# Scratch reads issued one unit behind the next write, and two norms ahead of two transposes, in a spectral filter with a gated MLP

## The chip, the cores and the metric

The kernel runs on one core of a Trainium2 chip. The metric is the device time of one execution in microseconds. The core has five instruction queues: PE (TensorE, matmuls), DVE (VectorE), ACT (ScalarE), POOL (GpSimd) and SP (SyncE, which here only issues DMAs). Each queue executes its own instructions in order and waits on semaphores for the others. An instruction that waits holds up everything behind it on its queue, also DMAs that have nothing to wait for.

## The reference

An input x of 2048 rows and 512 columns is layer-normed, and two branches of the normed input are added to x: a filter in the frequency domain (two-dimensional real FFT, product with complex weights, inverse FFT) and an MLP with a gated GELU of width 1792.

```python
def _A_ref(x, w_r, w_i):
    B, S, D = x.shape
    X = jnp.fft.rfft2(x.astype(jnp.float32), axes=(-2, -1))
    X = X * (w_r + 1j * w_i)
    return jnp.fft.irfft2(X, s=(S, D), axes=(-2, -1)).astype(jnp.bfloat16)

def _B_ref(x, w_gate, w_up, w_down):
    g = jnp.einsum("bsd,df->bsf", x, w_gate)
    u = jnp.einsum("bsd,df->bsf", x, w_up)
    h = _gelu(g) * u
    return jnp.einsum("bsf,fd->bsd", h, w_down)

x = A_x
xn = _layernorm(x, axis=-1)
return x + _A_ref(xn, A_w_r, A_w_i) + _B_ref(xn, B_w_gate, B_w_up, B_w_down)
```

## The kernel before

The rows are handled as 16 tiles of 128, in four blocks b of four tiles. The MLP is the backbone of TensorE's program: for each block and each of 14 chunks fc of the width there are a gate group (L685, four matmuls), an up group (L700, four matmuls), a GELU on ACT (L688) and a product on DVE (L706) into hT. The down products (L738, 14 matmuls for a tile) of a block run between the groups of the next block.

The spectral branch is threaded into this backbone by hand. A counter of hooks runs along the MLP groups; plan maps a hook's number to calls, and at(h, call) enters one. When the MLP loop reaches a hook, the calls of that number write their instructions into the queues. So the order within every queue is the order of the hooks, and all queues see the same order. PSUM banks are given out by take, from modelled times of TensorE and ACT.

The spectral branch has these stages. D units (the FFT over columns) and A units (first half of the FFT over rows) write their result to scratch memory in DRAM (scr1), and load_tv reads it back transposed into tv. Eight B units (the second half of the FFT, L570), each with a product with the filter weights W on DVE (L581), are followed by eight C units (first half of the inverse over rows, L595). A C unit ends with an eviction on ACT (L600) into one of two buffers vp, and a DMA on SP that writes vp to the scratch tensor scr2 (256 KB, L602). load_vv(g) (L605) is the DMA on SP that reads unit g back into vv, in the order that the last stage needs; vv lies in the same memory as the matrices of the first stages, the arena. It waits for its own unit's write to have landed. Every E unit (the second half of the inverse over rows, L619) needs all eight parts of vv. F units (L649), the inverse over columns, follow, and the results are added to x_sb and written out.

B unit g stands at hook 60 + 4.6 g, rounded down, and C unit g - 1 at the same hook. The E units begin at hook 113.

SP also issues the loads of the imaginary filter weights W_i in that stage (L337, function load_late): eight units, four DMAs for each, with W buffers for four units; those of the last four units fall among the C units (hooks 67, 68, 72, 73, 76, 77, 81, 82). Each waits for TensorE's progress at its hook and for the multiplies that last read the buffer. A small side path, mini, treats column 256; its step 3 at hook 100 sends a 4 KB row to scratch position z256 by a DMA on SP.

At the start, x tiles and the first weights come in by DMAs on the SP and ACT queues, which wait for nothing. The first two tiles are handled singly, so that the first gate can begin early: ln_stat and ln_aggr (statistics on DVE, a power on POOL with the constant tile mhalf, L388), ln_norm (L392, DVE) into xn, and trans1: for each half of the columns two transposes on TensorE (L832) and a copy from PSUM into xnT, the first half on DVE (L839), the second on ACT (L841). The first gate reads both tiles of xnT.

Of the kernel before, what the change touches and what calls it, by code (L numbers as in the profile page):

```python
# [11 lines left out]
F32 = mybir.dt.float32  # L12
# [6 lines left out]
P = 128  # L19
# [195 lines left out]
def bass_parallel_sum__spectral_gfnet__glu_gated_geglu__prompt_kernel(  # L215
# [27 lines left out]
    with ExitStack() as es:  # L243
        def sb(name, shape, dt):
            return es.enter_context(nc.sbuf_tensor(name, shape, dt))
# [50 lines left out]
        gl = [sb("gl%d" % i, [P, 512], BF16) for i in range(3)]  # L296
        st = sb("st", [P, NJ, 6], F32)
        ag = sb("ag", [P, NJ, 2], F32)
        vpe = sb("vpe", [P, NJ], F32)
        mhalf = sb("mhalf", [P, 4], F32)  # L300
        rstd = sb("rstd", [P, NJ], F32)
        dumm = sb("dumm", [P, 512], F16)
        warm_o = sb("warm_o", [P, 1], F32)
# [7 lines left out]
        def bank_h(i):  # L311
            return psum_h[:, i * 1024:(i + 1) * 1024]
# [8 lines left out]
        def take(n, dur, hold=None, ops=1):  # L321
            i = min(range(9 - n), key=lambda i: max(free[i:i + n]))
            pt[0] += dur
            if hold is None:
                act_t[0] = max(act_t[0], pt[0] + 0.25) + 0.2 + 0.43 * n
                end = act_t[0]
            else:
                end = pt[0] + hold
            for k in range(i, i + n):
                free[k] = end  # L330
            return i
# [50 lines left out]
        def ln_aggr(j0, n):  # L382
            for j in range(j0, j0 + n):
                op("dve", lambda e, j=j: e.bn_aggr(ag[:, j, :], st[:, j, :]), r=[("st", j)], w=[("ag", j)])
            sl = slice(j0, j0 + n)
            js = range(j0, j0 + n)
            op("dve", lambda e: e.tensor_scalar(vpe[:, sl], ag[:, sl, 1], LN_EPS, None, ALU.add), r=[("ag", j) for j in js], w=[("vpe", j) for j in js])  # L387
            op("pool", lambda e: e.tensor_tensor(rstd[:, sl], vpe[:, sl], mhalf[:, 0:n], ALU.pow), r=[("vpe", j) for j in js] + ["mhalf"],  # L388
               w=[("rstd", j) for j in js])

        def ln_norm(j):
            op("dve", lambda e: e.tensor_scalar(xn[:, j % 4, :], x_sb[:, j, :], ag[:, j, 0:1], rstd[:, j:j + 1], ALU.subtract, ALU.mult),  # L392
               r=[("x", j, 0), ("x", j, 1), ("ag", j), ("rstd", j)], w=[("xn", j % 4)])
# [365 lines left out]
        def at(h, *calls):  # L759
            plan.setdefault(int(h), []).extend(calls)  # L760
# [40 lines left out]
        for m in range(4):  # L801
            h = (11, 22, 31, 39)[m]
# [6 lines left out]
        for g in range(9):  # L809
            h = int(60 + 4.6 * g)  # L810
            if g < 8:
                at(h, (unit_B, g))
            if g > 0:
                at(h, (unit_C, g - 1))
                at(h + 3, (load_vv, g - 1))
            if g == 1:
                at(h, (mini, 1))
            if g == 8:
                at(h - 2, (mini, 4))
                at(h, (mini, 2))  # L820
        at(100, (mini, 3))
        for j in range(NJ):
            at(113 + 2.2 * j, (unit_E, j))
            at(117 + 2.2 * j, (unit_F, j))

        def trans1(j):
            for i, eng in enumerate(("dve", "act")):
                bk = take(1, 0.12, 1.0)
                def f(e, i=i, bk=bk):
                    ins = None  # L830
                    for a in range(2):
                        ins = e.transpose(bank_h(bk)[:, a * P:(a + 1) * P], xn[:, j, (2 * i + a) * P:(2 * i + a + 1) * P], ident[:])  # L832
                    return ins
                op("pe", f, r=["ident", ("xn", j)], w=[("ps", bk)])
                dst = xnT[:, 2 * i:2 * i + 2, j * P:(j + 1) * P]
                src = bank_h(bk)[:, 0:256].rearrange("p (a c) -> p a c", a=2)
                ks = [("xnT", 0, 2 * i + a, j) for a in range(2)]
                if eng == "dve":
                    op("dve", lambda e, dst=dst, src=src: e.tensor_copy(dst, src), r=[("ps", bk)], w=ks)  # L839
                else:  # L840
                    op("act", lambda e, dst=dst, src=src: e.activation(dst, src, ACT.Copy), r=[("ps", bk)], w=ks)  # L841
# [3 lines left out]
        ln_stat(1)  # L845
        ln_aggr(0, 2)
        ln_norm(0)
        trans1(0)
        ln_norm(1)
        trans1(1)  # L850
        gate(0, 0, (0, 1))
        ln_stat(2)
# [82 lines left out]
```

## Time and profile before

| | us |
|---|---|
| median of five runs | 189.76 |
| lowest and highest of the five | 188.70, 193.11 |
| the profiled execution: its own time | 189.76 |
| the profiled execution: span of the profile | 188.0 |

The granted TensorE clock was 1.00 in every stretch read. The stretches around the change:

| stretch, us | what runs in it | PE busy, us | ACT busy, us | DVE busy, us | DMA share |
|---|---|---|---|---|---|
| 6.5 to 8.5 | norm and transposes of the first two tiles | 0.78 | 0.77 | 0.90 | 1.09 |
| 8.5 to 13.5 | first gates and ups | 4.09 | 1.92 | 3.84 | 1.11 |
| 76 to 96 | B and C units, first half | 20.00 | 10.21 | 11.10 | 0.75 |
| 96 to 110 | B and C units | 14.00 | 7.46 | 7.61 | 0.86 |
| 110 to 122 | last B and C units | 11.95 | 6.58 | 5.74 | 0.72 |
| 122 to 134 | MLP alone, last scratch write and read | 12.00 | 3.25 | 4.31 | 0.47 |
| 134 to 181 | E and F units | 47.00 | 23.36 | 33.62 | 0.17 |

The busy time of an engine is the time that its records cover. Matmuls are pipelined, so their records overlap. The DMA share is the mean busy share of the core's 16 DMA engines; it can exceed 1 where packets of several queues overlap. In the lines of a timeline the first number is the start, the second the length, then the engine and line, what is written from what, and the number of instructions; a bracket gives the idle time of the engine ahead of it and what ended it. SPq is the issue of a DMA by SP, not its transfer.

### The profile page before, as it was taken

Reading aid. Unit: us, or ns where it says so; the run is one execution under the profiler, and the core shown is the slowest. Engines: PE = TensorE matmul, PEld = TensorE weight load, DVE = VectorE, ACT = ScalarE, POOL = GpSimd, SP = SyncE. Lnnn points to the kernel's source line nnn. Section 1 sums busy time; section 2 is a strip of 40 time slices with the busy share of each in tenths; the row PEclk is TensorE's granted clock in tenths of the full one; section 3 lists DMA queues with packets and bytes.
Section 4 is the critical chain, followed back from the end, with each engine's and each line's share of the span. In section 5 each row is a group of like instructions: output and inputs, shape, how many; then the busy total and the mean of one; then the engine's idle time right before and its main releaser. Section 6 shows DMA issues by size and latency. Waiting matters only on the chain.

```text
span 188.0 us, 3473 instructions
## 1 busy us (share of the span) xinstructions
PE 179.4 (95%) x1284; PEld 95.4 (51%) x1284; DVE 110.9 (59%) x262; ACT 88.8 (47%) x143; POOL 40.8 (22%) x90
## 2 busy tenths in 40 slices
PE   7589999999999999999999999999999999999991
PEld 2368655565655444444444444444555555555460
DVE  3566989997352242446635555423259879699520
ACT  1334547766566431456734555413265566654100
POOL 2110081824000007634654311000011111110000
PEclk9999999999999999999999999999999999999999
DMA  4999999788979249658988977664002212211111
GB/s 123 278 236 287 316 253 303 222 158 150 189 108 165 43 107 148 132 140 197 192 137 168 146 139 128 115 120 99 4 0 56 56 45 70 58 36 25 28 42 42
DMA packets 24977, 24.71 MB, mean 131 GB/s; under 512 B 2832, under 2 KB 22800, under 8 KB 24704
## 3 DMA queue, kind: packets, MB, share of 16 engines
q1 hardware_dynamic: 20992, 18.24, 47.2%
q0 software_dynamic: 1968, 5.14, 11.6%
q10 hardware_dynamic: 2000, 1.11, 2.2%
q8 instruction: 10, 0.16, 0.4%
q14 instruction: 7, 0.06, 0.1%
HBM read 18.19 MB, written 6.29 MB: 130 GB/s over the span
## 4 chain that ended last, share of the span: by engine, by line
PE 67%; DMA 16%; DVE 8%; SPq 4%; issue 2%; ACT 2%; POOL 1%; DVEq 0%; ACTq 0%
PE ps L738 21%; PE ps L700 18%; PE ps L685 17%; DMA scr<-early 10%; DMA wu<-in_B_w_up_dram 5%; DVE st L380 3%; SPq L334 2%; PE ps L649 2%; PE ps L619 2%; SPq L337 2%; DVE hT L706 1%; PE ps L402 1%; DMA out_dram<-x_sb 1%; ACT early L600 1%; PE ps L471 1%
## 5 line engine op out<-in xcount | busy, mean ns | idle before, releaser
L706 DVE TENSOR_TENSOR hT<-ps,gl 128x512 bf16<-128x512 f32 (+1 forms) x62 | 39.2, 637 | 34.5 <-PE ps L700 26.4
L700 PE MATMUL ps<-xnT,wu 128*128 128x512 f16 (+1 forms) x248 | 58.6, 359 | 1.0 <-DMA wu<-in_B_w_up_dram 0.9
L685 PE MATMUL ps<-xnT,wg 128*128 128x512 f16 (+1 forms) x248 | 58.6, 359 | 0.6 <-ACT xnT L841 0.6
L688 ACT ACTIVATE gl<-ps 128x512 bf16<-128x512 f32 (+1 forms) x62 | 34.3, 556 | 42.5 <-PE ps L685 41.3
L738 PE MATMUL ps<-wd,hT 128*128 128x512 bf16 x210 | 49.1, 380 | 0.0
L685 PEld LDWEIGHTS ps<-xnT,wg 128*128 128x128 bf16 x248 | 23.4, 98 | 21.7 <-issue 1.9
L700 PEld LDWEIGHTS ps<-xnT,wu 128*128 128x128 bf16 x248 | 23.4, 98 | 21.3 <-DMA wu<-in_B_w_up_dram 1.2
L738 PEld LDWEIGHTS ps<-wd,hT 128*128 128x128 bf16 x210 | 19.7, 98 | 21.9 <-issue 1.0
L640 DVE TENSOR_TENSOR x_sb<-ps,x_sb 128x512 bf16<-128x512 f32 (+1 forms) x17 | 11.2, 660 | 20.9 <-PE ps L738 17.5
L337 POOL DMA_DIRECT2D W<-in_A_w_r_dram x32 | 18.6, 612 | 12.0 <-PE ps L685 7.8
L628 POOL COPY tv<-tv 1x128 bf16<-1x128 bf16 x16 | 4.5, 284 | 51.7 <-ACT tv L626 51.7
L581 DVE TENSOR_TENSOR early<-early,W 128x1024 bf16<-128x1024 f16 x16 | 10.4, 688 | 6.8 <-ACT early L576 6.8
L655 ACT ACTIVATE tv<-ps 128x512 bf16<-128x512 f32 x16 | 9.5, 595 | 9.8 <-PE ps L649 9.8
L380 DVE BATCH_NORM_STATS2 st<-x_sb 128x6 f32<-128x512 bf16 x16 | 10.5, 683 | 2.9 <-DMA x_sb<-in_A_x_dram 2.9
L447 ACT ACTIVATE early<-ps 128x512 f16<-128x512 f32 x16 | 9.5, 595 | 5.4 <-PE ps L443 5.4
L576 ACT ACTIVATE early<-ps 128x1024 f16<-128x1024 f32 x8 | 8.2, 1023 | 6.1 <-PE ps L570 6.1
L626 ACT ACTIVATE tv<-ps 128x512 bf16<-128x512 f32 x16 | 9.6, 598 | 3.0 <-PE ps L619 3.0
L600 ACT ACTIVATE early<-ps 128x1024 bf16<-128x1024 f32 x8 | 8.2, 1022 | 4.6 <-DMA scr<-early 4.6
L479 ACT ACTIVATE early<-ps 128x1024 f16<-128x1024 f32 x8 | 7.9, 1021 | 4.6 <-PE ps L474 3.8
L388 POOL TENSOR_TENSOR rstd<-vpe,mhalf 128x4 f32<-128x4 f32 (+1 forms) x5 | 4.5, 901 | 23.5 <-DVE vpe L387 23.5
L559 POOL COPY w<-W 128x4 bf16<-128x4 bf16 x16 | 5.2, 355 | 14.4 <-DMA W<-in_A_w_i_dram 14.4
L392 DVE TENSOR_SCALAR cmx<-x_sb,ag,rstd 128x512 f16<-128x512 bf16 x16 | 6.2, 423 | 2.1 <-POOL rstd L388 2.1
(75 smaller groups left out, 147.5 us busy)
## 6 DMA issues: line engine op xcount, KB each, us to landing
W<-in_A_w_r_dram POOLq DMA_DIRECT2D x32, 64.2 KB, 3.9
W<-in_A_w_i_dram SPq DMA_DIRECT2D x32, 64.2 KB, 4.7
tv<-scr SPq DMA_DIRECT2D x8, 256.0 KB, 5.5
scr<-early SPq DMA_DIRECT2D x8, 256.0 KB, 4.2
arena<-scr SPq DMA_DIRECT2D x8, 256.0 KB, 4.3
out_dram<-x_sb SPq DMA_DIRECT2D x30, 64.0 KB, 2.0
scr<-early SPq DMA_DIRECT2D x14, 128.0 KB, 3.4
x_sb<-in_A_x_dram SPq DMA_DIRECT2D x6, 256.0 KB, 11.9
```

The costliest lines, as they stand in the source:

```text
L337: op(eng, lambda e: e.dma_start(dst, src), w=list(keys) + list(also), dma=True, after=[("pe", pr.cnt["pe"])])
L380: op("dve", lambda e: e.bn_stats(st[:, j, :], x_sb[:, j, :]), r=[("x", j, 0), ("x", j, 1)], w=[("st", j)])
L447: op("act", lambda e: e.activation(x4.rearrange("p (a c r) -> p a c r", a=2, r=4), bank(bk).rearrange("p (a r c) -> p a c r", a=2, r=4), A ...
L581: op("dve", lambda e, k=k: e.tensor_tensor(pp[i][k], xc[i], W[k][g % 4][:, :, :, 0:256], ALU.mult), r=[("xc", i)] + [key for c in range(2) ...
L600: op("act", lambda e: e.activation(vp[i].rearrange("p c hh k -> p (c hh k)"), pair(bk), ACT.Copy), r=[("ps", bk), ("ps", bk + 1)], w=[("vp ...
L626: op("act", lambda e: e.activation(z, bank(bk).rearrange("p (a c) -> p a c", a=4), ACT.Copy, scale=SC_E), r=[("ps", bk)], w=[zk] + (TVK if ...
L640: op("dve", lambda e: e.tensor_tensor(x_sb[:, j, cs], src, x_sb[:, j, cs], ALU.add), r=r + [("acc", j), ("x", j, 0), ("x", j, 1)], w=[("ac ...
L685: ins = e.matmul(bank(bg)[:, 0:n], wg_sb[:, dc, fc * P:(fc + 1) * P], xnT[:, dc, c0:c0 + n], start=(dc == 0), stop=(dc == 3))
L688: op("act", lambda e: e.activation(gl[k % 3][:, 0:n], bank(bg)[:, 0:n], ACT.Gelu_apprx_tanh), r=[("ps", bg)], w=[("gl", k % 3)])
L700: ins = e.matmul(bank(bu)[:, 0:n], wu_sb[:, dc, fc * P:(fc + 1) * P], xnT[:, dc, c0:c0 + n], start=(dc == 0), stop=(dc == 3))
L706: op("dve", lambda e: e.tensor_tensor(hT[b % 2][:, fc, h0:h0 + n], bank(bu)[:, 0:n], gl[k % 3][:, 0:n], ALU.mult), r=[("ps", bu), ("gl", k ...
L738: ins = e.matmul(bank(bk), hT[b % 2][:, fc, jj * P:(jj + 1) * P], wd_sb[:, fc, :], start=(fc == 0), stop=(fc == NFC - 1))
```

## The change

Three edits. The allocation of the small tile mhalf moves ahead of that of vpe. In the plan, the read of unit g - 1 at three hooks behind C unit g - 1 goes; in its place the read of unit g - 2 is entered at the hook of C unit g - 1, after it, and the read of the last unit is entered at hook 101. At the start, ln_norm(1) is issued ahead of trans1(0).

```diff
@@ -296,8 +296,8 @@
         st = sb("st", [P, NJ, 6], F32)
         ag = sb("ag", [P, NJ, 2], F32)
+        mhalf = sb("mhalf", [P, 4], F32)
         vpe = sb("vpe", [P, NJ], F32)
-        mhalf = sb("mhalf", [P, 4], F32)
         rstd = sb("rstd", [P, NJ], F32)
@@ -812,13 +812,15 @@
                 at(h, (unit_B, g))
             if g > 0:
                 at(h, (unit_C, g - 1))
-                at(h + 3, (load_vv, g - 1))
+                if g > 1:
+                    at(h, (load_vv, g - 2))
             if g == 1:
                 at(h, (mini, 1))
             if g == 8:
                 at(h - 2, (mini, 4))
                 at(h, (mini, 2))
         at(100, (mini, 3))
+        at(101, (load_vv, 7))
         for j in range(NJ):
             at(113 + 2.2 * j, (unit_E, j))
             at(117 + 2.2 * j, (unit_F, j))
@@ -845,8 +847,8 @@
         ln_stat(1)
         ln_aggr(0, 2)
         ln_norm(0)
+        ln_norm(1)
         trans1(0)
-        ln_norm(1)
         trans1(1)
         gate(0, 0, (0, 1))
         ln_stat(2)
```

## The prediction

> **What bounds the kernel now.** I read the busy shares first, then the slices of the span.
>
> ```profile
> PE 179.4 (95%) x1284; PEld 95.4 (51%) x1284; DVE 110.9 (59%) x262; ACT 88.8 (47%) x143; POOL 40.8 (22%) x90
> ...
> PE   7589999999999999999999999999999999999991
> ```
>
> TensorE is busy everywhere but in the first 14 us and the last 6. Matmul records overlap, so a busy row can hide small holes. I therefore looked for holes in the distance between starts in TensorE's timeline: four 512-column matmuls of a gate or up group take 0.86 us from start to start of the next group. After 8.5 us, four gate or up groups end in a wait: 1.11 us at 12.45, 0.39 at 25.9, 0.23 at 33.8 and 0.22 at 120.3. The change can only win what it takes out of these, out of the 8.5 us ahead of the first gate, or out of the tail.
>
> Then the chain that ended last, which seems to contradict this:
>
> ```profile
> PE 67%; DMA 16%; DVE 8%; SPq 4%; issue 2%; ACT 2%; POOL 1%; DVEq 0%; ACTq 0%
> PE ps L738 21%; PE ps L700 18%; PE ps L685 17%; DMA scr<-early 10%; DMA wu<-in_B_w_up_dram 5%; DVE st L380 3%; SPq L334 2%; PE ps L649 2%; PE ps L619 2%; SPq L337 2%; DVE hT L706 1%; PE ps L402 1%; DMA out_dram<-x_sb 1%; ACT early L600 1%; PE ps L471 1%
> ```
>
> It gives 10% (18.5 us) to the scratch writes of the inverse. This follows one release, of 0.22 us, back through a string of transfers that ran beside a full TensorE. The 18.5 us are what the string lasts, not what it costs. SP's timeline shows why it is a string: each read (arena<-scr) waits for the write just ahead of it to land, and the next write stands behind that read.
>
> ```profile
> 115.21 0.42 SPq L334 DMA_DIRECT2D scr<-early  x1
> 119.40 0.30 SPq L334 DMA_DIRECT2D arena<-scr  x1
> 119.75 0.42 SPq L334 DMA_DIRECT2D scr<-early  x1
> 124.05 0.30 SPq L334 DMA_DIRECT2D arena<-scr  x1
> 124.40 0.42 SPq L334 DMA_DIRECT2D scr<-early  x1
> 128.56 0.30 SPq L334 DMA_DIRECT2D arena<-scr  x1
> ```
>
> One turn is 4.5 us. What it delays: ScalarE may not evict a C unit (L600) until the write of two units earlier has landed; it waits three times, 4.6 us in all, and TensorE feels only the last, for a PSUM bank.
>
> ```profile
> ACT early L600 <- DMA scr<-early: 4.6, 3, 2.6
> ...
> 119.47 1.03 PE L685 MATMUL ps<-xnT,wg 128*128 128x512 f16 x4
> 120.55 1.04 PE L700 MATMUL ps<-xnT,wu 128*128 128x512 f16 x4
> ```
>
> 1.08 - 0.86 = **0.22 us**. And the last read, issued at 128.56, takes 4.4 us, so it lands at 132.96; the first E unit loads its weights at 133.13. The string ends 0.17 us before TensorE needs it.
>
> **Part 1, the reads one unit behind.** Eight reads (0.31 us of SP each) and eight writes stay; no instruction is added. The read of unit g-1, which stood three hooks behind its write, now stands behind the write of unit g, a full turn of 4 or 5 hooks (about 5 us) later, and waits for a write that is by then mostly down. SP's queue is then write 1, read 0, W loads, write 2, read 1, and so on. Working it out from ScalarE's L600 starts plus 1.02 us: write 3 can go at 99.6 (before: 104.2), write 4 at 105.0 (111.3), write 7 at about 118.7 (124.4). Read 7 now also stands behind the z256 row's DMA, whose row is ready at 121.96, and needs write 7 landed: 118.7 + 4.2 = 122.9. It lands at 127.3, **5.8 us** ahead of the first E unit instead of 0.17. L600 loses its 4.6 us of waits. The gain at TensorE is the 0.22 us alone: next late is TensorE itself.
>
> Moved past: the two W_i loads at hooks 68, 73, 77 and 82 no longer queue behind a read that waits for a fresh write. They issue up to some 4 us earlier (today the second pair for unit 6 issues at 101.9, behind the read at 101.56, and GpSimd's copy of it waits until 109.3). They keep their own waits: TensorE's progress and the multiplies that free the W buffers. None of today's multiplies (L581) is put down to a W load in the waits, so that is worth nothing at TensorE. A read that still waits would hold up the next write and W pair on SP; that is less than today's full landing each time. The first read overwrites the arena's matrices, last read at 62.7, so it waits for nothing there.
>
> Two rules of the Trainium skill differ from rows here. "DMA: Bandwidth & Descriptors", Anatomy of one DMA, fits a transfer (on GpSimd's path) at 2.0 us plus its bytes at 436 GB/s. My estimate from it is 2.6 us for 256 KB; a turn would be about 3.3 us, SP would always be back in time, and this part would gain 0. The rows have 2.6 to 5.4 us for these writes, six of eight above 4, so I take the row: 0.22. The same page, Issuing engines are not separate DMA queues, speaks against the change: all queues run on the same 16 engines and interleave, so a read let loose beside a write brings no bandwidth, and both may land later. At worst, both landings double. The stretches of the windows view say how near that is: DMA share 0.86 at 96 to 110, 0.72 at 110 to 122, 0.47 at 122 to 134. The end decides, where there is room, so I take no growth, and keep doubling for the rival below.
>
> **Part 2, both norms ahead of the transposes.** Two DVE instructions swap with one copy; nothing is added. Today DVE runs norm 0, copy, norm 1, copy:
>
> ```profile
> 6.03 0.41 DVE L392 TENSOR_SCALAR cmx<-x_sb,ag,rstd 128x512 f16<-128x512 bf16 x1 [0.85 <-POOL rstd L388]
> ...
> 7.11 0.40 DVE L392 TENSOR_SCALAR cmx<-x_sb,ag,rstd 128x512 f16<-128x512 bf16 x1
> ```
>
> Two norms in a row take 0.83 us (the pair at 24.33), so norm 1 ends at 6.86 instead of 7.51. Transposes follow 0.15 later, 7.0 to 7.4; ScalarE's second copy (0.38) runs 7.43 to 7.81, and the first gate, 0.15 behind it, starts at 7.96 instead of 8.53: **0.57 us**. TensorE then runs into the weights. A gate or up group of 256 columns takes 0.435. The third gate could start at 9.70, but its weights, issued at 3.19, land after 6.7 us, at 9.9; the fifth gate's land at 4.12 + 7.6 = 11.7. And the fifth up:
>
> ```profile
> 12.02 0.60 PE L685 MATMUL ps<-xnT,wg 128*128 128x256 f16 x4
> 13.56 0.61 PE L700 MATMUL ps<-xnT,wu 128*128 128x256 f16 x4 [0.94 <-DMA wu<-in_B_w_up_dram]
> ```
>
> It waits for wu 4 to 6, issued at 4.67, landed at 13.51. These loads wait for no computation, so nothing in this part moves them. The hole grows from 1.11 us to about 1.4, and **0** of the 0.57 is left. If the cover is gone, all 0.57 comes through. The swapped 16- and 64-byte allocations move two small operands of five pow instructions; no row prices an address. Between 0 and, say, doubling the one pow on the chain (1.02 us at 23.29), I take 0, since the instructions keep shape and type.
>
> **Sum.** The profiled execution took 189.76 us: 188.0 of span and 1.76 around it. 188.0 - 0.22 - 0 = 187.8; with 1.76, **189.5 us**. Its 189.76 is also the median of the five runs, which spread from 188.70 to 193.11. I count 0.5% (0.95 us) as what a measurement of this kernel can tell from no change.
>
> **Rivals.**
>
> *A typical execution waits where this one just doesn't* (faster; 0.35). The string's end had 0.17 us to spare, and from 96.26 to 132.96 it consists almost wholly of landings. If these are 4% longer in another execution, the string ends 1.5 us later and TensorE waits 1.3 us at the first E unit. The change takes this wait away. For it: the spread of the five times, two of them above 192. Against it: the profiled execution has the median's time with no such wait, and the spread can as well come from the weight loads at the start. Its time: the lowest of the five, with the least waiting, less 0.22: 188.5.
>
> *The start's gain comes through* (0.10). 189.76 - 0.22 - 0.57 = 189.0, still within 0.5%. It needs wu 4 to 6 landed before 12.1 us; DMA share is above 1 from 6.5 to 13.5, which speaks against it.
>
> *The freed transfers crowd each other* (slower; 0.05). At 118.7 write 7 goes, and the first E unit starts 133.1 - 118.7 = 14.4 us later; write and read need 8.6 us today. Above 14.4, that is at 1.7 times today's landings, TensorE waits for the difference: doubled, 17.2 us, 2.8 us late, 189.76 - 0.22 + 2.8 = 192.3. The DMA share of 0.47 there speaks against it.
>
> *Something else makes it slower by over 0.5%* (0.06): an address, or later weight landings, about 191.
>
> *No gain that shows*, my forecast: 0.44.
>
> **How the numbers follow.** Faster 0.35; same 0.44 + 0.10 = 0.54; slower 0.05 + 0.06 = 0.11. Predicted 189.5. The range runs from 187.8 (the first rival with another 0.4%) to 190.6 (the forecast plus 0.6% of spread), which leaves the slower cases out. The forecast's own range is 188.6 to 190.4.
>
> **What would show it.** Right: writes and reads alternate on SP with reads of the unit before, write 7 issues near 119, the last read lands near 127, L600's wait for scr is gone, and the 0.22 us hole at 120.3 with it; the first gate starts near 8.0 and the fifth up still near 13.5. Wrong: landings of scr above 7 us in the changed kernel, a hole ahead of the first E unit, a fifth up much before 13.2, or a median gain above 1 us, which would mean that the profile before was a lucky execution.

## The result, and the profile after

The changed kernel takes 188.87 us (median of 40 runs, 187.85 to 190.05); the kernel before, in the same comparison, 189.66 us (77 runs, 188.62 to 193.11). The ratio is **0.9962, with a 95% interval of 0.9948 to 0.9976**: 0.7 us less, between 0.45 and 1.0. Ratios here and below leave out the executions that are more than 1.5% above the fastest of the same kernel. The forecast was a gain of 0.2 us, within the 0.5% that the text called no change; the measured one (0.4%) stays within it too, but is three times as large and clear of nothing.

The profiled execution of the changed kernel has a span of 187.2 us and a time of 188.97. Its busy shares and slices:

```profile
PE 180.1 (96%) x1284; PEld 95.5 (51%) x1284; DVE 110.8 (59%) x262; ACT 88.9 (47%) x143; POOL 39.7 (21%) x90
...
PE   7889999999999999999999999999999999999991
```

TensorE is the bound as before. The chain that ended last has lost its scratch writes:

```profile
PE 81%; DVE 8%; DMA 6%; SPq 2%; issue 2%; POOL 1%; ACT 0%; DVEq 0%
PE ps L738 25%; PE ps L700 22%; PE ps L685 21%; DMA wu<-in_B_w_up_dram 4%; DVE st L380 3%; SPq L334 2%; PE ps L595 2%; PE ps L619 2%; PE ps L649 2%; PE ps L570 1%; DVE hT L706 1%; PE ps L402 1%; DMA out_dram<-x_sb 1%; PE ps L471 1%; PE ps L721 1%
```

The 10% that stood at "DMA scr<-early" are now TensorE's, and the span is 0.8 us shorter, not 18.5: the share said what the string lasted. SP's timeline at the end of the inverse (start, length of the issue, what is issued):

```profile
118.25 0.36 SPq L334 DMA_DIRECT2D scr<-early  x1
118.65 1.25 SPq L334 DMA_DIRECT2D arena<-scr  x1
121.22 0.59 SPq L334 DMA_DIRECT2D tv<-row  x1
121.86 0.58 SPq L334 DMA_DIRECT2D arena<-scr  x1
```

The last write goes at 118.25 and the last read at 121.86; with its 4.4 us it lands at 126.3, and the first E unit loads its weights at 132.33. No wait of the evictions L600 for scr is listed any more, and TensorE's timeline runs through where the hole was:

```profile
ACT early L600 <- PE ps L595: 0.8, 1, 0.8
...
118.92 1.03 PE L685 MATMUL ps<-xnT,wg 128*128 128x512 f16 x4
119.78 1.03 PE L700 MATMUL ps<-xnT,wu 128*128 128x512 f16 x4
```

0.86 us from start to start, where it was 1.08. At the start of the kernel:

```profile
7.81 0.60 PE L685 MATMUL ps<-xnT,wg 128*128 128x256 f16 x4 [0.59 <-ACT xnT L843]
...
13.00 0.61 PE L700 MATMUL ps<-xnT,wu 128*128 128x256 f16 x4 [0.90 <-DMA wu<-in_B_w_up_dram]
```

The fifth up still waits for its weights, but these landed at 13.0, not at 13.5. The span fell by 0.8 us: 0.56 at the fifth up and 0.22 at the hole. Are these 0.56 us the change's doing, or the luck of one execution?

For the profiles below the span can be taken apart in the same way. From the start of the fifth up to the end, 174.2 us pass where no wait for SP's string is left in TensorE's timeline: 174.20 in the changed kernel (187.2 - 13.00), and 174.1 to 174.3 in the other profiles without such a wait and with the same tail. What a profile has above that agrees to about a tenth with the holes that end in such a wait. So each profile gives two numbers, the start of the fifth up and what is above 174.2, here called the string's toll.

### The profile page after: what moved, and what is told of

The parts are those of the page before. It is cut to its first block, busy times and chain, and to the rows that moved or that the text cites. A ratio compares the mean times of both kernels' runs of the same rounds, so it can differ in the third digit from the quotient of the medians.

```text
span 187.2 us, 3473 instructions
## 1 busy us (share of the span) xinstructions
PE 180.1 (96%) x1284; PEld 95.5 (51%) x1284; DVE 110.8 (59%) x262; ACT 88.9 (47%) x143; POOL 39.7 (21%) x90
## 4 chain that ended last, share of the span: by engine, by line
PE 81%; DVE 8%; DMA 6%; SPq 2%; issue 2%; POOL 1%; ACT 0%; DVEq 0%
PE ps L738 25%; PE ps L700 22%; PE ps L685 21%; DMA wu<-in_B_w_up_dram 4%; DVE st L380 3%; SPq L334 2%; PE ps L595 2%; PE ps L619 2%; PE ps L649 2%; PE ps L570 1%; DVE hT L706 1%; PE ps L402 1%; DMA out_dram<-x_sb 1%; PE ps L471 1%; PE ps L721 1%
## 5 line engine op out<-in xcount | busy, mean ns | idle before, releaser
L600 ACT ACTIVATE early<-ps 128x1024 bf16<-128x1024 f32 x8 | 8.2, 1020 | 0.8 <-PE ps L595 0.8
L640 DVE TENSOR_TENSOR x_sb<-tv,x_sb 128x512 bf16<-128x512 bf16 x16 | 6.8, 425 | 0.6
```

The source lines that it names most:

```text
L640: op("dve", lambda e: e.tensor_tensor(x_sb[:, j, cs], src, x_sb[:, j, cs], ALU.add), r=r + [("acc", j), ("x", j, 0), ("x", j, 1)], w=[("ac ...
```

## The experiments

**Each part alone, and the kernel before once more.** Three runs with one part each, and one of the kernel before, unchanged:

```diff
# reads_only
-                at(h + 3, (load_vv, g - 1))
+                if g > 1:
+                    at(h, (load_vv, g - 2))
...
         at(100, (mini, 3))
+        at(101, (load_vv, 7))
# norms_only
-        trans1(0)
         ln_norm(1)
+        trans1(0)
# alloc_only
+        mhalf = sb("mhalf", [P, 4], F32)
         vpe = sb("vpe", [P, NJ], F32)
-        mhalf = sb("mhalf", [P, 4], F32)
```

> The kernel before with the moved scratch reads alone. Theory S (the start's gain comes through in most executions, the reads give what the hole at 120.3 had): 0.2 us less than before, a ratio near 0.999, the hole at 120.3 gone, wu 4 to 6 awaited as before. Theory R (most executions wait in the inverse stage longer than the profiled one, and the reads take that away): 0.6 to 0.7 us less, a ratio near 0.9965. Theory A (the addresses of two small tiles): 0.2 us less, as under S.

> The kernel before with both norms ahead of the transposes alone. Theory S: about 0.5 us less, a ratio near 0.9972; the first gate near 7.9 and the fifth up nearer to 13.0 than to 13.5. Theory R: no difference in the time, ratio 1.000, the first gate near 7.9 and the fifth up at about 13.5. Theory A: no difference.

> The kernel before with the allocation of mhalf ahead of that of vpe alone. Theories S and R: no difference, ratio 1.000. Theory A: some 0.5 us less, ratio near 0.997.

> The kernel before, unchanged, as a second sample of its profile and as a measure of what a comparison can tell. All theories: ratio 1.000. Theory R expects a profile in which the first E unit or a C unit's eviction costs TensorE more than the 0.22 us of the first profile; theory S expects about 0.2 us there again, and a landing of wu 4 to 6 that differs from 13.5 by some tenths.

| kernel | median, us | ratio to before, 95% interval | time of the profiled execution | fifth up starts | string's toll |
|---|---|---|---|---|---|
| before | 189.66 | | 189.76 | 13.56 | 0.24 |
| reads alone | 189.14 | 0.9965, 0.9942 to 0.9987 | 189.17 | 13.20 | 0 |
| norms alone | 190.12 | 1.0016, 0.9986 to 1.0047 | 190.53 | 13.05 | 1.45 |
| allocation alone | 189.41 | 0.9987, 0.9962 to 1.0012 | 190.01 | 13.72 | 0.28 |
| before, again | 189.72 | 0.9995, 0.9969 to 1.0022 | 188.90 | 12.79 | 0.1 |
| both parts | 188.87 | 0.9962, 0.9948 to 0.9976 | 188.97 | 13.00 | 0 |

Theory R has the better of it: the moved reads alone have a gain clear of nothing (0.25 to 1.1 us), and at its central value it is the whole of it. Theory S, in the form in which the norms give half a microsecond by themselves, fails in the time, though it had the start right (the fifth up nearer to 13.0). That they give something once the reads are moved is left open by it. Theory R missed on the second profile of before: it expected a toll above 0.22, and there is about 0.1 and no hole near 120. The allocation shows no effect.

The spread gives a hint how the reads gain. In before, a tenth of the executions lie below 188.84 and a tenth above 190.80; with moved reads the two bounds are 188.80 and 190.40, and the median is 0.5 us lower. The best executions are as they were, the middle and the long ones are shorter. This fits a string that takes something in some executions and nothing in others. Two columns of the table say more on the start. The fifth up starts between 12.79 and 13.72 without the norms' change, so the 13.00 of the changed kernel is within what the weights' landing does from one execution to the next. In the second profile of before, the weights, issued at 4.7, had landed after 7.9 us, by 12.6, and the fifth up did not wait at all:

```profile
12.35 0.60 PE L685 MATMUL ps<-xnT,wg 128*128 128x256 f16 x4
12.79 0.60 PE L700 MATMUL ps<-xnT,wu 128*128 128x256 f16 x4
```

Then TensorE itself is the limit, and an earlier first gate would pay.

The surprise is in the profile of the norms alone. Its fifth up is half a microsecond earlier than in the first profile, and it loses more than that near 120. TensorE's timeline there, then SP's where the string falls behind:

```profile
119.33 1.03 PE L685 MATMUL ps<-xnT,wg 128*128 128x512 f16 x4
121.34 0.82 PE L700 MATMUL ps<-xnT,wu 128*128 128x512 f16 x3 [0.99 <-ACT early L600]
```

```profile
102.83 1.00 SPq L334 DMA_DIRECT2D scr<-early  x1
103.93 1.26 SPq L337 DMA_DIRECT2D W<-in_A_w_i_dram  x2
110.37 0.31 SPq L334 DMA_DIRECT2D arena<-scr  x1
```

Write 3 was issued 1.4 us earlier than in before (102.83 against 104.20), yet the read that waits for it stands at 110.37 instead of 109.66. All later writes are late by about that, the evictions on ScalarE wait 7.6 us for scr instead of 4.6, and the hole that this tears in TensorE is 1.15 us instead of 0.22. The rest of the toll of 1.45 is a second hole: the late eviction also holds up the GELU behind it on ScalarE, and a C unit that waits for this starts at 112.59, 0.34 us after TensorE could have started it.

```profile
ACT early L600 <- DMA scr<-early: 7.6, 3, 3.1
...
112.01 0.41 PE L570 MATMUL ps<-tv,be 64*64 64x256 f16 x8
112.59 0.63 PE L595 MATMUL ps<-early,cmx 64*64 64x256 bf16 x16 [0.16 <-ACT gl L688]
```

**The norms alone, once more.** The same edit, to see whether that was one execution.

> The norms alone once more, for a second profile and a larger sample. Theory T (the span is the start of the fifth up, plus a constant, plus what SP's string of writes and reads takes from TensorE; the norms pay only where the weights land early): fifth up near 13.0, no hole near 120 as large as the 1.15 us of the first profile, a time between 0 and 0.4 us below the kernel before, and a few executions below 188.6. Theory G (the string gives back what the start gains): a hole near 120 above 0.5 us again, no execution below 188.6, ratio 1.000 or above.

189.48 us, ratio 0.9991 (0.9961 to 1.0021). Its profile is nearly the same, line by line: write 3 at 102.88, its read at 110.35, and near 120:

```profile
119.30 1.03 PE L685 MATMUL ps<-xnT,wg 128*128 128x512 f16 x4
121.19 1.04 PE L700 MATMUL ps<-xnT,wu 128*128 128x512 f16 x4 [0.86 <-ACT early L600]
```

The fifth up at 13.02, a toll of 1.4. No execution of the 14 was below 188.6, and none of the 14 of the first run. Theory T, which expected no such hole and a few executions below 188.6, fails. Theory G fits both profiles: with the reads where they were, the string gave back what the start had gained. Both profiled executions are above the medians of their runs (190.53 against 190.12, 190.42 against 189.48), so a typical toll is smaller. Nor does an earlier start always bring a hole: the second profile of before started its fifth up earlier still, at 12.79, and had none. Why write 3 lands so late when the norms are moved was not settled; the string's toll may depend on how its transfers meet the W loads around 102 to 110, but no run shows it.

**A third eviction buffer.** If the toll is the C unit's eviction, which waits for a buffer, a third buffer takes it away without touching the reads.

```diff
# vp3
+        vp.append(sb("vp2", [P, 1024], BF16)[:].rearrange("p (c hh k) -> p c hh k", c=2, hh=2))
...
-            op("act", lambda e: e.activation(vp[i]...), r=[...], w=[("vp", i)])
+            op("act", lambda e: e.activation(vp[g % 3]...), r=[...], w=[("vp", g % 3)])
...
-            dma("sp", ..., vp[i]..., r=[("vp", i)], w=[("scr2", g)])
+            dma("sp", ..., vp[g % 3]..., r=[("vp", g % 3)], w=[("scr2", g)])
# vp3_late: as vp3, and
-            at(113 + 2.2 * j, (unit_E, j))
-            at(117 + 2.2 * j, (unit_F, j))
+            at(115 + 2.2 * j, (unit_E, j))
+            at(119 + 2.2 * j, (unit_F, j))
# before_E_first: the kernel before, and
-            at(113 + 2.2 * j, (unit_E, j))
-            at(117 + 2.2 * j, (unit_F, j))
+            at(111 + 2.2 * j, (unit_E, j))
+            at(115 + 2.2 * j, (unit_F, j))
```

> The kernel before with a third buffer for the evictions of the C units, reads as before. Theory C (what typical executions lose is TensorE's wait for a bank that a C unit's late eviction holds, near 120): L600 no longer waits for scr, the hole near 120 is gone, and most of the gain of the moved reads is there, 0.4 to 0.7 us, ratio 0.9965 to 0.998. Theory E (they lose it at the first E unit, which waits for the last read): SP's string of writes and reads is as long as before, so no gain, ratio 1.000, and a wait ahead of the first E unit in some executions.

189.54 us against 189.53, ratio 1.0006 (0.9978 to 1.0034). In the profile the hole near 120 is gone, and so is the toll; the last read is issued at 128.16, nearly as late as before, from a first write at 96.34 (before: 96.26), so the string is about as long as it was. Its fifth up starts at 14.14, later than in any other profile with this order of loads. The gain of 0.4 us or more that theory C asked for isn't there, and neither is the wait at the first E unit that theory E expected in some executions. That is the other place where the string can take its time, so I tried both edges:

> The kernel before with a third eviction buffer and the E and F units two hooks later, reads as before. Theory O (the string takes its time from TensorE at two places, the C unit's late eviction near 120 and the first E unit; with one closed it takes it at the other): with both closed the gain of the moved reads is there, 0.5 to 0.7 us, ratio about 0.9965. Theory E0 (the string takes nothing that these two places can show, and the moved reads gain elsewhere): ratio 1.000, as with the third buffer alone.

> The kernel before with the E and F units two hooks (one gate and one up, 1.73 us) earlier. Theory O: the last read lands when it did, so TensorE waits ahead of the first E unit for 1.2 to 2.5 us, and the time rises by about that much, ratio 1.006 to 1.013. Theory E0 (the first E unit had room to spare in typical executions): a wait of at most 1 us, ratio below 1.004.

The third buffer with later E units: 189.30 us against 189.80, ratio 0.9993 (0.9960 to 1.0026). Both 0.9965 and 1.000 lie in that interval; it doesn't tell the two theories apart. Its profile has neither a hole near 120 nor a wait at the first E unit.

E units two hooks earlier: 191.13 us, **ratio 1.0058 (1.0026 to 1.0090)**, 1.1 us more (0.5 to 1.7) for 1.73 us of advance. That lies between what the two theories called for, at the lower edge of theory O. My estimate from it is that in a typical execution of before the string ended about 0.6 us ahead of the first E unit (1.73 - 1.1), with an interval of 0 to 1.2 us, if the wait there is all that the earlier units cost; the first profile had 0.17. The profiled execution of this run took 192.55 us, 1.4 above the median; it shows where the string bites, not how hard in a typical execution:

```profile
121.93 1.04 PE L700 MATMUL ps<-xnT,wu 128*128 128x512 f16 x4 [1.36 <-ACT early L600]
132.10 1.03 PE L700 MATMUL ps<-xnT,wu 128*128 128x512 f16 x4
134.37 0.38 PE L619 MATMUL ps<-be,arena 128*128 128x128 f16 x4 [1.24 <-DMA arena<-scr]
```

The second wait is made by the edit. The first isn't: at 121.9 the kernel is still instruction for instruction the one before. So a long execution of before can have a hole of 1.5 us there. The other four profiles with the old reads, the old eviction and the old norms (before, before again, allocation alone, and the one with early weights below) had 0.22, 0, 0.31 and 0, the two with the norms alone 1.15 and 1.03. The profiles with moved reads, five of them with those below, have none near 120 and none at the first E unit.

**The cover at the start.** The norms' gain was to be hidden by the weights of chunks 4 and 5. I tried to bring these in earlier, half of them on ACT's queue:

```diff
# before_early, reads_early, after_early
             load_w(t, v, nm, 2, 4, eng)
+            load_w(t, v, nm, 4, 6, eng)
...
-        load_w(wg_sb, wgv, "wg", 4, 6, "sp")
-        load_w(wu_sb, wuv, "wu", 4, 6, "sp")
```

> The kernel before with the weights of chunks 4 and 5 issued right behind those of 2 and 3, half of them on ACT's queue. Theory W (the fifth up waits for its weights in most executions): wu 4 to 6 lands before 12.5, the fifth up starts near 12.5, and the time falls by what the wait had, some 0.5 to 0.9 us. Theory G (the inverse's string of transfers is paced by itself, so an earlier start only makes the hole near 120 larger): no gain in the time, a hole larger by what the start gained.

> The moved reads and the early weights, norms as before. Theory W: the gains add up, 1.2 to 1.6 us less than before, ratio near 0.993. Theory G, since the string is gone here: the same.

> The changed kernel with the early weights. If the weights' landing is what covers the norms' gain, it shows here: up to 0.57 us less than the kernel with moved reads and early weights but norms as before, a ratio near 0.990, fifth up near 11.9. If the norms give nothing even without that cover, it is equal to that kernel.

| kernel | median, us | ratio to before, 95% interval | executions below 188.6 us |
|---|---|---|---|
| before + early weights | 190.21 | 1.0028, 1.0000 to 1.0055 | 0 of 22 |
| moved reads + early weights | 189.30 | 0.9988, 0.9966 to 1.0009 | 1 of 22 |
| both parts + early weights | 189.22 | 0.9980, 0.9957 to 1.0002 | 3 of 22 |
| both parts | 188.87 | 0.9962, 0.9948 to 0.9976 | 13 of 40 |
| moved reads | 189.14 | 0.9965, 0.9942 to 0.9987 | 0 of 22 |
| norms (both runs) | | | 0 of 28 |

The edit failed at what it was for. The weights didn't land earlier: in the profile of before with early weights the third up waits for wu and the fifth gate for wg, and the fifth gate starts at 13.35, where it was 12.02. The DMA engines were full there already (share 1.16 from 8 to 10 us and 1.07 from 10 to 13.4), and the new order moved the waits from one group to another. So the cover was never taken away, and theory W wasn't tested.

But the three kernels differ from each other by one part each, and that can be read. Moving the reads took 0.9 us here (190.21 to 189.30; the two intervals overlap only between 1.0000 and 1.0009), which is the second comparison in which the moved reads gain. Where they gain is again not seen: the profile of before with early weights has no hole near 120. Moving the norms as well gave nothing that shows (189.30 to 189.22). The last column says more on the norms. Of the kernels with the old norms not one execution is below 188.6 us (0 of the 77 of before, 0 of 22 with moved reads), but for one of 22 with early weights. With both parts there are 13 of 40. An estimate from the profiles fits that: nine groups of 0.435 us behind the first gate (8.53 and 7.81), the fifth up can start at 12.45 in before and at 11.73 in the changed kernel; with 174.2 and the 1.77 us around the span that is 188.4 and 187.7 us, and the fastest executions took 188.62 and 187.85. So in the executions in which the weights land early, TensorE's own start would be the limit, and there the earlier first gate comes through; none of these executions was profiled. With the old reads the norms give no such executions (0 of 28). How much the norms add to the reads in the median was not resolved: the medians differ by 0.27 us, which is less than the intervals.

**A version that beats both.** The chain of both kernels ends in a wait: the second half of the last tile is added to x_sb only when the first half has left for the output, because both halves carry one key. They touch different columns.

```diff
# after_tail: the changed kernel, and
-  r=r + [("acc", j), ("x", j, 0), ("x", j, 1)], w=[("acc", j)])
+  r=r + [("acc", j), ("x", j, 0), ("x", j, 1)], w=[key or ("acc", j)])
...
-                add_to(NJ - 1, bank(bc)[:, 0:256], [("ps", bc)], cs)
+                add_to(NJ - 1, bank(bc)[:, 0:256], [("ps", bc)], cs, ("half", c))
...
-  dma(eng, ov[b, :, NJ - 1, cs], ..., r=[("acc", NJ - 1)], w=[("out", NJ - 1, b, c)])
+  dma(eng, ov[b, :, NJ - 1, cs], ..., r=[("half", c)], w=[("out", NJ - 1, b, c)])
```

> The changed kernel with separate keys for the two halves of the last tile, so that the second addition to x_sb no longer waits for the first half's transfer to the output. In the profile that wait is 2.2 us, of which 0.8 would be TensorE's own work anyway. All theories: 0.9 to 1.2 us less than the changed kernel, a ratio near 0.991 to the kernel before.

188.01 us, **ratio 0.9906 (0.9868 to 0.9943)**, 0.86 us below the median of the changed kernel, just under the 0.9 to 1.2 expected. The last addition, in the changed kernel and then here (the bracket names what it waited for):

```profile
184.21 0.42 DVE L640 TENSOR_TENSOR x_sb<-ps,x_sb 128x256 bf16<-128x256 f32 x1 [2.22 <-DMA out_dram<-x_sb]
```

```profile
183.21 0.42 DVE L640 TENSOR_TENSOR x_sb<-ps,x_sb 128x256 bf16<-128x256 f32 x1 [1.10 <-PE ps L721]
```

Now TensorE itself releases it. Unlike the string's toll, this wait stands in all 13 profiles of kernels that share the key, with 2.2 us in each.

## Why the prediction was right, and where it was too small

**The bound and the chain.** Right. TensorE is full from the first gates to the tail, and taking the 18.5 us of scratch writes out of the chain gained 0.7 us.

**Part 1's mechanism.** Right, in order and nearly in time. Write 3 was expected at 99.6 and stood at 99.00, write 4 at 105.0 and 104.42, write 7 at 118.7 and 118.25, all early by about what the start had gained. The last read was to be ready to go at 122.9 and went at 121.86; its lead on the first E unit was to be 5.8 us and is 6.1. The evictions' waits for scr went from 4.6 us to none.

**Part 1's size.** This is the term that failed: "The gain at TensorE is the 0.22 us alone". It took the hole of one execution for the hole of a typical one. The moved reads alone measured a ratio of 0.9965, 0.7 us (0.25 to 1.1). That the forecast still held is due to the width of its own 0.5%, not to the size of this term. Profiles of the same stretch with the old reads show holes between 0 and 0.31 us with the old norms, 1.03 and 1.15 with the new ones, and 1.5 in a long execution. The first kind alone doesn't make up 0.7 us; the lower end of the interval would fit it, and the rest must lie in executions that weren't profiled or in what the norms add, so how the 0.7 us of the whole change divide stays open. The moved reads also let the loads of W_i go out earlier, and no run separates this from the evictions; in no profile does TensorE wait for a product with these weights. The first rival named the size: a string that ends with 0.17 us to spare takes time in other executions. It was right that the toll differs between executions, and for all that the profiles show it put the wait in the wrong place: it named the first E unit, and in every profile with the E units where they were and a wait at all, this came from the late evictions of the C units, near 120 and in two also at 112.6. At the first E unit a typical execution had some 0.6 us to spare (0 to 1.2). That this is the next edge is shown by moving the units; that the third buffer gave nothing because the wait only went on to there is a guess that its profile, with no wait at either place, doesn't support.

**The transfers crowding each other.** In the changed kernel the DMA share at 96 to 110 is 1.12 instead of 0.86, and landings of writes and reads from 96 to 125 reach 8.6 us, where 5.4 and 5.3 were the longest. This agrees with what the Trainium skill says in "DMA: Bandwidth & Descriptors", Issuing engines are not separate DMA queues: all queues run on the same 16 engines. Landings above 7 us were named as a sign of being wrong, and they came; but no wait of TensorE for them is left in the profile, because there are now several microseconds for each. At the end, where it would have counted, the last read took 4.4 us, as before. The estimate of 2.6 us for 256 KB from the same page, Anatomy of one DMA, fits the shortest writes only (2.5 to 2.7 us); the row was the right basis.

**Part 2.** The first gate was expected at 7.96 and started at 7.81 in the changed kernel. The cover did what the prediction said: the fifth up waits for its weights in the profile, 1.07 us instead of the expected 1.4, because they landed half a microsecond earlier than in before (13.0; a start much before 13.2 was to be a sign of being wrong). The cover is not there in every execution, as the second profile of before shows and the 13 executions below 188.6 us suggest. And the prediction had no term for the granted clock: executions with a low one all but vanish with the moved norms (the last section). So the worth of this part is above the 0 that I took, by an amount that the runs don't fix. That the norms alone would give their gain back near 120 I hadn't seen at all; the sum treated the parts as independent.

**The allocation.** Nothing shown, as expected.

## What to carry to other kernels

A transfer chain that ends a few tenths ahead of the engine that bounds the kernel can cost more than one profile shows: here the profile had 0.22 us, and moving the reads alone took out 0.25 to 1.1. So look for strings where every transfer waits for the last one, and profile the same kernel more than once before pricing them. Two changes along one path aren't priced apart: an earlier start upstream can be taken back by a chain of transfers downstream, as in both profiles of the norms alone. A dependency kept for a whole tile, when the two halves don't overlap, is worth looking for at the end of the path, where it stood in every profile here. And compare the granted clocks of all executions beside their medians; here they show an effect that the medians hide.

## What was unexpected of the hardware

In the one profile of the kernel with moved reads and early weights, the first gate started at 9.17, later than in the others. From 10 to 13.4 its granted TensorE clock was 0.54, and groups of four 256-column matmuls stood 0.85 us apart instead of 0.43:

```profile
10.36 1.06 PE L684 MATMUL ps<-xnT,wg 128*128 128x256 f16 x4
11.21 1.06 PE L699 MATMUL ps<-xnT,wu 128*128 128x256 f16 x4
12.07 1.06 PE L684 MATMUL ps<-xnT,wg 128*128 128x256 f16 x4
```

That cost some 1.6 us, about four groups at 0.4 each. TensorE had done little but eight transposes between the end of its warm-up matmuls at 6.7 and the first gate. The other thirteen profiles have the first gate between 7.81 and 8.86, and a clock of 1.00 throughout from 6 to 13.4.

This execution was not alone. The mean granted clock over the span is on record for 426 executions, and it falls into two groups, 0.994 to 1.000 and 0.979 to 0.991; this profile has 0.986. With the norms where they were, 64 of 326 executions are in the lower group; with both norms ahead of the transposes, 2 of 100. Where a kernel has both groups among the executions that the ratios count, the median of the lower one is 0.9 to 1.8 us longer. So the moved norms take away most of these executions. An estimate of what this is worth is a fifth of the executions times some 1.3 us, about 0.25 us in the mean, of which a median shows little. It fits that the earlier first gate prevents the dip, but only this one execution of the lower group was profiled, so where the others lost their clock is not shown, and a later first gate alone was not tried.

The moved reads leave the dip as it was (8 of 44 executions with the old norms), so their gain is another matter. Without the lower group, and among the executions that the ratios count, their medians are 189.04 us against 189.38 for before, and 189.09 against 190.04 with early weights.
